# A hashed attention with a max-of-three feed-forward: new costs in the build-time planner, and weights sent on other queues

## The chip, the core and the metric

The kernel runs on one core of a Trainium2 chip. The core has a matrix engine (TensorE, PE in the profile, with its weight loads as PEld), a vector engine (VectorE, DVE), an activation engine (ScalarE, ACT), GpSimd (POOL) and SyncE (SP), which here only issues DMA transfers. Each engine runs its own instructions strictly in the order in which the program holds them, and waits for the others by semaphores. An instruction that waits therefore holds up everything behind it on its engine. DMA transfers are issued from the queue of SyncE, ACT or POOL. The metric is the time of one execution in microseconds (us), as the median of several runs.

## The reference

Two computations follow each other. The first is attention with a hashed mask: a key counts for a query only if six sign bits agree.

```python
q_bits = (np.einsum('bhsd,dk->bhsk', q, proj) > 0)      # q, k, v: 4 x 8 x 768 x 64
k_bits = (np.einsum('bhsd,dk->bhsk', k, proj) > 0)      # proj: 64 x 6
q_bucket, k_bucket = sum(q_bits * powers), sum(k_bits * powers)
mask = q_bucket[:, :, :, None] == k_bucket[:, :, None, :]
scores = np.where(mask, q @ k.T / 8, -1e9)
attn = softmax(scores)
x = (attn @ v)        # heads side by side: 3072 tokens x 512
h = np.maximum(np.maximum(x @ w1, x @ w2), x @ w3)      # w1, w2, w3: 512 x 768
out = h @ w_out                                          # w_out: 768 x 512
```

All inputs and the output are float32. Where no key shares a query's bucket, the softmax is over equal values, so that the mean of v is what is left; the kernel adds a tiny share of that mean everywhere.

## The kernel before

**Tiles and stages.** A batch b has eight heads, handled in four pairs. A pair is written (b, pr) here, so (1,3) is the fourth pair of the second batch. For each pair the kernel loads q, k and v (`load`, 384 KB each), splits q and k into a half-precision part and its remainder (`split_h`, `split_r`), and brings both into the layout that scores need, the tile T. Batch 0 and the first two pairs of batch 1 do this with TensorE (`pe_T`, `evac_T`), all others with one transposing DMA from SyncE (`xbar`, L271). From T come the sign bits: small matmuls with the projection (`hash_mm`, L298 or L300), a comparison (`hash_bits`), a transpose of the bits (`bit_T`, `bit_evac`), and a round trip through DRAM (`bit_out` L337, `bit_in` L340) that writes the bits as extra rows into T. These rows, scaled by a large number, act as the mask inside the score matmul itself. A pair's scores can thus start only after its `bit_in` has landed.

The attention of one head and half a sequence takes three units, each of two score matmuls (`score`, L383), one exponential on ACT (`expo`, L389) and six matmuls with v (`attend`, L401). Division and placement are DVE's (`norm_t` L418, `norm_x` L437). `mean_mm` (L361, L364) makes the mean of v. For b = 0 it sums the half-precision v; for later batches POOL sums v first (`vsum`, L351 to L354). `vcast` makes v half-precision, for batch 0 on POOL (L193), later on ACT (L191).

The feed-forward works on half a batch, (b, hf). The half's x is transposed (by TensorE for the first half, else by one transposing DMA, `x_bar`, L445). Then come 18 groups of four matmuls (`l1`, L466), whose results ACT and DVE take from PSUM (`l1_evac`, L191, L193, L475), and three chunks of six matmuls with w_out (`l2`, L480), each copied (`l2_evac`) and stored (`store`, L489). This work fills TensorE while ACT works on the exponentials of the following batches, and what is left runs on its own at the end.

**Weights.** w1, w2, w3 are loaded by casting DMAs from POOL's queue, half by half (`load_w`, L523), w_out by one such DMA (L638). `weights` gives their places: the first halves early, the second half of w1 after pair (0,3), of w2 and w3 after pair (1,0), w_out after pair (1,1). A `hold` instruction on POOL makes them wait until that pair's bit rows have landed.

**The order of the work.** It is not written by hand. `Plan.run` simulates the engines while the program is built: every step has engines with costs, a priority (mostly the number of the unit that needs it), dependencies and the buffers that it takes and gives back. At each moment a free engine takes the ready step with the lowest priority number, and the step's instructions are emitted in that order. DMA transfers stand in one queue: a transfer occupies it for `xfer` us, after the issuing engine's cost and a lead time, and counts as landed 1.2 us after that. A transposing DMA costs SyncE 2.0 us (`xbar`) or 1.4 us (`x_bar`), with 4.3 or 2.1 us of queue. Where the planner is wrong, the order stays as it was built, and the engines wait.

**Gates and buffers.** The loads of later pairs are also gated: they are planned after the `bit_in` of a given earlier pair (`g` in `prep`). The pools that matter are T (8 buffers, pool `opnd`), the output tiles (3, `osb`), the exponentials (5, `at`) and three PSUM banks (`mm`) that nearly all other matmuls share.

Of the kernel before, what the change touches and what calls it, by code (L numbers as in the profile page):

```python
# [18 lines left out]
class Task:  # L19
    def __init__(self, kinds, prio, deps, emit, take=(), give=(), after=(), lat=0.0, xfer=0.0):  # L20
        self.kinds, self.prio, self.emit = kinds, prio, emit
        self.deps = [d for d in deps if d is not None]
        self.take, self.give, self.lat, self.xfer = take, give, lat, xfer
        self.after = [t for t in after if t is not None]
        self.start = None


class Plan:
# [17 lines left out]
    def run(self):  # L46
# [11 lines left out]
        while n < len(self.tasks):  # L58
            moved = True
            while moved:  # L60
                moved = False
                for e in engines:
# [22 lines left out]
                    events.append((busy[e], -1, None))  # L85
                    if t.xfer:
# [16 lines left out]
            while queue and queue[0][0] < 1e-6:  # L103
                t = queue.pop(0)[1]
                events.append((now + POST, t.n, t))
            events.sort(key=lambda x: x[:2])
            while events and events[0][0] <= now:
                at, kind, t = events.pop(0)
                if kind == -2:
                    queue.append([t.xfer, t])  # L110
                    continue
# [12 lines left out]
def kernel(  # L124
# [39 lines left out]
    OSB = 3  # L164
# [4 lines left out]
    opnd = ctx.enter_context(tc.tile_pool(name="opnd", bufs=8))  # L169
# [5 lines left out]
    hp = ctx.enter_context(tc.tile_pool(name="hp", bufs=HT))  # L175
    op = ctx.enter_context(tc.tile_pool(name="op", bufs=OSB))
# [7 lines left out]
    plan = Plan({"sc": 2, "av": 1, "mm": 3, "at": 5, "q": 4, "k": 4, "v": 4, "s": 4, "T": 8,  # L184
                 "xn": XN, "xT": XT, "ht": HT, "osb": OSB, "bit": 2, "bt": 2, "dr": 4, "t": 2})
# [102 lines left out]
    def hash_mm(b, pr, heads, e):  # L288
        hps = bank(("h", b, pr), "hps")
        K = NBITS if b == 0 else 2 * NBITS  # L290
        for n in range(2):
            for hh in range(*heads):
                for c in range(NCH):
                    a = n * NA2 + hh * NCH + c
                    o = hps[:, a * K : (a + 1) * K]
                    if b == 0:
# [179 lines left out]

    def l2(b, hf, c, e):
        ps = bank(("o", b, hf, c), "po")
        for fb in range(NF):
            nc.tensor.matmul(ps[:], hts[b, hf, fb][:, c * P : (c + 1) * P], wout_sb[:, fb, :],  # L480
                             start=fb == 0, stop=fb == NF - 1)

    def l2_evac(b, hf, c, e):
        osbs[b, hf, c] = op.tile([P, DM], FP32, tag="osb", name="osb")
        copy(e, osbs[b, hf, c][:], pss.pop(("o", b, hf, c))[:])

    def store(b, hf, c, e):
        rows = out[b * S : (b + 1) * S, :].rearrange("(p c) m -> p c m", c=NCH)
        nc.sync.dma_start(rows[:, hf * CH + c, :], osbs.pop((b, hf, c))[:])  # L489
# [36 lines left out]
    last_load, last_copy = [None], [None]  # L526
    bounced = {}

    def value(b, pr, dep):
# [5 lines left out]
        else:  # L535
            ready_v[b, pr] = add(("ACT", 0.72), U - 6, [dep, prev], lambda e: vcast(b, pr, e))
# [5 lines left out]
    def prep(b, pr):  # L542
# [3 lines left out]
        if b > 0:  # L546
            for n in "qkv":
                g = divmod(4 * b + pr - GATE, 4)
                if b == 1:
                    g = {("q", 0): (0, 2), ("k", 0): (0, 2), ("q", 2): (1, 0), ("k", 2): (1, 0), ("v", 2): (1, 0)}.get(  # L550
                        (n, pr), (0, 3) if pr < 2 else (1, 1))
                loads[n, b, pr, (0, 2)] = add(("SP", 0.5), U - 44 + 0.1 * "qkv".index(n), [],
                                              lambda e, n=n: load(n, b, pr, (0, 2), e), take=(n,), xfer=1.1,
                                              after=[last_load[0], bounced[g]])
# [46 lines left out]
        if not by_pe:  # L601
            ev = [add(("SP", 2.0), p0 + 2, both_rs, lambda e: xbar(b, pr, e), xfer=4.3, take=("T",))]
        plan.join(ev, ("s",))
        hm = add(("PE", 1.3 if b == 0 else 0.67), p0 + 4, ev + [mp], lambda e: hash_mm(b, pr, (0, 2), e), take=("mm",))
        hb = add(("DVE", 0.3 if b == 0 else 0.62), p0 + 5, [hm],
                 (lambda e: hash_bits(b, pr, e)) if b else (lambda e: hash_bits0(pr, (0, 2), e)), take=("bit",), give=("mm",))
# [22 lines left out]

    def weights(b, pr, parts):  # L630
        if pr or b:
            prev = add(("POOL", 0.1), -150, [bounced[b, pr]], lambda e: hold(b, pr, e), after=[wprev[0]])
        else:
            prev = ready_v[0, 1]
        for w in parts:
            if w == "o":
                prev = add(("POOL", 0.8), -90, [],
                           lambda e: nc.gpsimd.dma_start(wout_sb[:], moe_w_out.rearrange("(c p) m -> p c m", p=P)),  # L638
                           xfer=4.6, after=[prev])
# [6 lines left out]
    stage = {(0, 3): [(1, 0)], (1, 0): [(1, 1), (1, 2)], (1, 1): ["o"]}  # L646

    def ffn(b, hf, deps):
# [16 lines left out]
        for c in range(CH):  # L665
# [94 lines left out]
```

The softmax here doesn't subtract the row's maximum and nothing guards it: scores larger than these inputs give would overflow.

## Time and profile before

| | |
|---|---|
| median of 6 runs | 275.71 us (274.5 to 277.77) |
| the profiled execution | 274.5 us |
| its span, first to last instruction | 272.7 us |
| TensorE busy | 259.9 us, 95% |
| ACT busy | 195.9 us, 72% |
| DVE busy | 175.0 us, 64% |
| POOL busy | 38.6 us, 14% |
| mean granted TensorE clock | 0.990 |
| moved by DMA | 40.51 MB, in 67,216 packets |

The profile is of one execution. Busy time of TensorE is not time at its peak, since matmuls overlap: the start of one 384-column matmul to the next is 162 ns in dense stretches, while a group's mean length is given as 327. A DMA share can exceed 1 in the table of stretches; read it as a queue that is never empty. SyncE has no busy time of its own: its timeline shows how long each issue held it. Of the words in a wait, the right side is what came last. The granted clock is the share of the full TensorE clock that the chip allows.

### The profile page before, as it was taken

What the parts mean: (1) busy time and instruction counts of PE and PEld (TensorE: products, weight loads), DVE (VectorE), ACT (ScalarE), POOL (GpSimd) and SP (SyncE); (2) the same over time, 40 slices, a digit from 0 to 9 for tenths busy, and PEclk for the clock granted to TensorE, in tenths of its full rate; (3) what the DMA queues carried; (4) which work ended last, traced back from release to release, by engine and by line L of the source; (5) the groups of instructions that cost most, each with busy time, mean ns of one, the idle gap of its engine ahead of it and who ended that gap; (6) DMA issues with size and microseconds to landing.
All of it is one profiled execution on the core that took longest, in us unless ns stands there. A gap on an engine that the chain in (4) does not pass through costs nothing.

```text
span 272.7 us, 7413 instructions
## 1 busy us (share of the span) xinstructions
PE 259.9 (95%) x3034; PEld 174.9 (64%) x3034; DVE 175.0 (64%) x392; ACT 195.9 (72%) x282; POOL 38.6 (14%) x56
## 2 busy tenths in 40 slices
PE   7899989999999699899999999999999999999993
PEld 7778767667656365567666676666666656565551
DVE  4898588959958578667999466464356715354350
ACT  5788899989856178899999889998889432322322
POOL 1170043604303033030333000000000000000000
PEclk9999999999999979999999999999999999999998
DMA  6995496799999979998899950211250060120303
GB/s 199 370 232 90 142 277 192 122 155 335 190 299 226 164 233 225 265 236 238 198 208 218 239 116 8 30 30 41 77 60 4 0 168 8 40 79 0 115 0 117
DMA packets 67216, 40.51 MB, mean 149 GB/s; under 512 B 47982, under 2 KB 64110, under 8 KB 67182
## 3 DMA queue, kind: packets, MB, share of 16 engines
q1 hardware_dynamic: 63150, 36.90, 55.3%
q0 software_dynamic: 3952, 3.15, 7.8%
q8 instruction: 23, 0.38, 0.6%
q14 instruction: 11, 0.09, 0.1%
q10 hardware_dynamic: 80, 0.00, 0.0%
HBM read 25.72 MB, written 6.84 MB: 119 GB/s over the span
## 4 chain that ended last, share of the span: by engine, by line
PE 75%; DMA 9%; DVE 7%; ACT 4%; issue 2%; SPq 1%; ACTq 0%
PE ps L466 32%; PE sc L383 19%; PE av L401 10%; PE po L480 10%; ACT AT L389 3%; DMA q<-in_q_dram 3%; DMA T<-s 3%; DVE s L262 3%; DMA T<-dr 3%; PE hps L300 2%; DVE s L257 2%; PE tps L281 1%; PE hps L298 1%; DVE T L193 1%; ACT s L255 1%
## 5 line engine op out<-in xcount | busy, mean ns | idle before, releaser
L389 ACT ACTIVATE AT<-sc 128x768 f16<-128x768 f32 x192 | 146.0, 812 | 16.0 <-PE sc L383 15.1
L466 PE MATMUL ps<-xT,w_sb 128*128 128x384 f16 x576 | 107.1, 327 | 0.7 <-ACT ht L191 0.6
L383 PE MATMUL sc<-T 128*128 128x384 f16 x384 | 93.8, 328 | 3.2 <-DMA T<-dr 1.9
L475 DVE TENSOR_TENSOR ht<-ht,ps 128x384 f16<-128x384 f16 x96 | 53.0, 552 | 47.0 <-PE ps L466 43.5
L401 PEld LDWEIGHTS <-AT 128*128 128x128 f16 x1152 | 60.1, 98 | 24.2 <-issue 1.1
L466 PEld LDWEIGHTS <-w_sb 128*128 128x128 f16 x576 | 52.4, 98 | 31.0 <-issue 1.5
L401 PE MATMUL av<-vone,AT 128*128 128x65 f16 x1152 | 66.3, 194 | 0.2 <-DVE t L418 0.2
L383 PEld LDWEIGHTS <-T 128*128 128x128 f16 x384 | 30.1, 97 | 14.2 <-DMA T<-dr 2.5
L191 ACT CAST ht<-ps 128x384 f16<-128x384 f32 x30 | 14.4, 478 | 32.8 <-DVE ht L475 20.6
L480 PE MATMUL po<-wout_sb,ht 128*128 128x512 f16 x144 | 33.4, 379 | 0.1
L191 ACT COPY osb<-po 128x512 f32<-128x512 f32 x23 | 13.5, 585 | 18.6 <-PE po L480 18.5
L480 PEld LDWEIGHTS <-ht 128*128 128x128 f16 x144 | 13.6, 98 | 14.7 <-issue 0.2
L351 POOL TENSOR_TENSOR vt<-v 128x384 f32<-128x384 f32 x12 | 13.4, 1117 | 63.5 <-DMA v<-in_v_dram 63.4
L418 DVE TENSOR_TENSOR t<-av,mv 128x390 f32<-128x390 f32 x32 | 17.9, 560 | 6.7 <-PE av L401 6.7
L262 DVE SCALAR_TENSOR_TENSOR s<-k,s 128x384 f16<-128x384 f32 x32 | 20.5, 653 | 0.7 <-ACT s L255 0.5
L262 DVE SCALAR_TENSOR_TENSOR s<-q,s 128x384 f16<-128x384 f32 x32 | 18.2, 582 | 3.3 <-ACT s L255 3.1
L193 DVE CAST ht<-ps 128x384 f16<-128x384 f32 x18 | 10.0, 555 | 15.1 <-PE ps L466 15.0
L437 DVE TENSOR_TENSOR xn<-t,rr 128x384 f16<-128x384 f32 x32 | 18.9, 591 | 1.1
L281 PE MATMUL tps<-iden,s 128*128 128x128 f16 x168 | 13.4, 219 | 1.6 <-DVE s L262 0.8
L281 PEld LDWEIGHTS <-s 128*128 128x128 f16 x168 | 10.4, 97 | 3.1 <-DVE s L262 2.2
L191 ACT CAST vone<-v 128x768 f16<-128x768 f32 x12 | 10.0, 837 | 0.3 <-DMA v<-in_v_dram 0.3
L300 PEld LDWEIGHTS <-T 128*128 128x128 f16 x288 | 8.7, 96 | 1.7 <-DMA T<-s 0.8
(53 smaller groups left out, 141.3 us busy)
## 6 DMA issues: line engine op xcount, KB each, us to landing
v<-in_v_dram SPq DMA_DIRECT2D x16, 384.0 KB
out_dram<-osb SPq DMA_DIRECT2D x24, 256.0 KB
q<-in_q_dram SPq DMA_DIRECT2D x15, 384.0 KB
k<-in_k_dram SPq DMA_DIRECT2D x15, 384.0 KB
w_sb<-in_moe_w_dram POOLq DMA_DIRECT2D x6, 384.0 KB, 6.8
wout_sb<-in_moe_w_out_dram POOLq DMA_DIRECT2D x1, 768.0 KB, 11.0
dr<-bt SPq DMA_DIRECT2D x15, 36.0 KB
T<-dr SPq DMA_DIRECT2D x15, 36.0 KB
```

The source lines that it names most:

```text
L191: nc.scalar.copy(o, i)
L262: nc.vector.scalar_tensor_tensor(out=s[:, a0:a1, D : 2 * D], in0=raw_view(n, b, pr, heads), scalar=QS, in1=s[:, a0:a1, 0:D], op0=AluOp.mul ...
L281: nc.tensor.transpose(p16[:, c * P : (c + 1) * P], S16[b, pr][:, a0 + c, :], iden[:])
L300: nc.tensor.matmul(o, T[b, pr][:, a, :], PAB[:], start=True, stop=True)
L383: nc.tensor.matmul(sc[:, i, 0:HQ], t[:, NA2 + hh * NCH + 2 * j + i, :], t[:, hh * NCH + hf * CH : hh * NCH + (hf + 1) * CH, :], start=True ...
L389: nc.scalar.activation(AT[:], scs.pop(u)[:, :, 0:HQ], ActFn.Exp, bias=EXP_BIAS, scale=EXP_SCALE)
L401: nc.tensor.matmul(av[:, o : o + D + 1], AT[:, i, c * P : (c + 1) * P], vones[b % 2][:, 2 * pr + hh, 2 * j + i, 0 : D + 1], start=slot == ...
L418: nc.vector.tensor_tensor(out=t[:, :, :, 0 : D + 1], in0=av[:, :, :, 0 : D + 1], in1=mv, op=AluOp.add)
L437: nc.vector.tensor_tensor(out=xv, in0=t[:, :, :, 0:D], in1=rr[:].to_broadcast([P, 2, CH, D]), op=AluOp.mult)
L466: nc.tensor.matmul(ps[:, 0:HQ], w_sb[i][:, jc, fb * P : (fb + 1) * P], xTs[b, hf][:, jc, :], start=jc == 0, stop=jc == NJ - 1)
L475: nc.vector.tensor_tensor(out=ht[:], in0=ht[:], in1=ps[:, 0:HQ], op=AluOp.max)
L480: nc.tensor.matmul(ps[:], hts[b, hf, fb][:, c * P : (c + 1) * P], wout_sb[:, fb, :], start=fb == 0, stop=fb == NF - 1)
```

## The change

The diff has six parts.

1. The planner knows a `hold`: a step with it keeps its engine (SyncE) until the transfer has reached the head of the queue and run for `hold` us. Transposes of T are now 0.6 us of issue, 3.4 of hold and 4.6 of queue, those of x 0.6, 1.0 and 2.3. Loads of a pair are planned only after the transpose of the pair two before it.
2. The gates of batch 1's loads move: those of pair (1,2) are now planned right behind those of (1,1). The second halves of w1 and w2 follow pair (0,3), that of w3 pair (1,0).
3. w_out is no longer cast by a DMA. SyncE loads it in three pieces of 512 KB in float32 into two new buffers (`wst`), and POOL casts them.
4. `vcast` of batch 1 is done by POOL instead of ACT.
5. The hash of pair (0,3) uses the form that batches 1 to 3 have: one matmul with both parts of the projection and a comparison of two columns, instead of two accumulating matmuls.
6. The last chunk of w_out is computed, copied and stored in two halves of 256 columns. T has 6 buffers instead of 8, and the output has 4 instead of 3.

```diff
@@ Plan.run
-                    events.append((busy[e], -1, None))
-                    if t.xfer:
+                    if t.hold:
+                        busy[e] = 1e9
+                        events.append((now + dur, -2, t))
+                    else:
+                        events.append((busy[e], -1, None))
+                    if t.hold:
+                        pass
+                    elif t.xfer:
...
-                t = queue.pop(0)[1]
+                t, hold = queue.pop(0)[1:]
+                if hold:
+                    busy[t.engine] = now
+                    queue.insert(0, [t.xfer - t.hold, t, 0.0])
+                    continue
...
-    OSB = 3
+    OSB = 4
-    opnd = ctx.enter_context(tc.tile_pool(name="opnd", bufs=8))
+    opnd = ctx.enter_context(tc.tile_pool(name="opnd", bufs=6))
+    wst = ctx.enter_context(tc.tile_pool(name="wst", bufs=2))
@@ hash_mm
-        K = NBITS if b == 0 else 2 * NBITS
+        summed = 4 * b + pr < 3
+        K = NBITS if summed else 2 * NBITS
@@ value
-            ready_v[b, pr] = add(("ACT", 0.72), U - 6, [dep, prev], lambda e: vcast(b, pr, e))
+            ready_v[b, pr] = add(("POOL", 0.9) if b == 1 else ("ACT", 0.72), U - 6, [dep, prev], lambda e: vcast(b, pr, e))
@@ prep
-                    g = {("q", 0): (0, 2), ("k", 0): (0, 2), ("q", 2): (1, 0), ("k", 2): (1, 0), ("v", 2): (1, 0)}.get(
-                        (n, pr), (0, 3) if pr < 2 else (1, 1))
+                    g = {("q", 0): (0, 2), ("k", 0): (0, 2)}.get((n, pr), (0, 3) if pr < 3 else (1, 0))
...
-                                              after=[last_load[0], bounced[g]])
+                                              after=[last_load[0], bounced[g], xbars.get(4 * b + pr - 2)])
...
-            ev = [add(("SP", 2.0), p0 + 2, both_rs, lambda e: xbar(b, pr, e), xfer=4.3, take=("T",))]
+            ev = [add(("SP", 0.6), p0 + 2, both_rs, lambda e: xbar(b, pr, e), xfer=4.6, hold=3.4, take=("T",))]
+            xbars[4 * b + pr] = ev[0]
@@ weights
+    def stage_w(w, i, e):
+        from_dram = w_view(w, i)[0]
+        t = wst.tile([P, 2 * DM], FP32, tag="ws", name="ws")
+        wst_tiles[w, i] = t[:, 0 : 2 * from_dram.shape[2]].rearrange("p (c f) -> p c f", c=2)
+        nc.sync.dma_start(wst_tiles[w, i], from_dram)
+
+    def cast_w(w, i, e):
+        copy(e, w_view(w, i)[1], wst_tiles.pop((w, i)))
...
-                prev = add(("POOL", 0.8), -90, [],
-                           lambda e: nc.gpsimd.dma_start(wout_sb[:], moe_w_out.rearrange("(c p) m -> p c m", p=P)),
-                           xfer=4.6, after=[prev])
+                for i in range(NF // 2) if w == "o" else range(NJ // 2):
+                    ld = add(("SP", 0.5), -60 if w == "o" else -70, [], lambda e, w=w, i=i: stage_w(w, i, e), take=("ws",),
+                             xfer=1.4 if w == "o" else 1.1, after=[prev])
+                    prev = ld
+                    parts.append(add(("POOL", 1.5 if w == "o" else 1.1), -60, [ld], lambda e, w=w, i=i: cast_w(w, i, e),
+                                     give=("ws",)))
...
-    stage = {(0, 3): [(1, 0)], (1, 0): [(1, 1), (1, 2)], (1, 1): ["o"]}
+    stage = {(0, 3): [(1, 0), (1, 1)], (1, 0): [(1, 2)], (1, 1): ["o"]}
@@ ffn
-        for c in range(CH):
+        for c in range(CH) if (b, hf) != (B - 1, 1) else (0, 1, 2.1, 2.6):
@@ main loop
-                    lst = [add(("SP", 1.4), u, lst, lambda e, b=b, hf=hf: x_bar(b, hf, e), xfer=2.1, take=("xT",),
+                    lst = [add(("SP", 0.6), u, lst, lambda e, b=b, hf=hf: x_bar(b, hf, e), xfer=2.3, hold=1.0, take=("xT",),
```

## The prediction

> **What bounds the kernel now.** I read four views in this order: busy time by engine, busy time by stretch, the SyncE timeline, the chain.
>
> ```profile
> PE 259.9 (95%) x3034; PEld 174.9 (64%) x3034; DVE 175.0 (64%) x392; ACT 195.9 (72%) x282; POOL 38.6 (14%) x56
> ```
>
> TensorE is the bound: 95% busy, and what it still lacks is the prize. Nothing after 120 us leaves it idle (below), so an idle microsecond removed before that is a microsecond off the end. The stretches (start:end, then busy us of PE, weight loads, DVE, ACT, POOL; granted clock; DMA share; GB/s) say where it idles:
>
> ```profile
> 24.00:60.00 36.00, 34.44 (x522) 25.43 (x519) 27.87 (x66) 33.80 (x48) 10.15 (x14) 1.00 0.71 162
> 60.00:88.00 28.00, 28.00 (x324) 18.39 (x323) 21.92 (x49) 21.94 (x32) 8.02 (x11) 1.00 1.13 262
> 88.00:96.00 8.00, 5.41 (x48) 3.07 (x46) 4.30 (x12) 0.96 (x2) 0.00 (x0) 1.00 1.08 182
> 96.00:100.00 4.00, 4.00 (x47) 2.52 (x45) 3.40 (x6) 2.81 (x5) 1.54 (x2) 0.58 0.52 161
> 100.00:116.00 16.00, 14.88 (x183) 9.51 (x181) 11.95 (x28) 13.92 (x20) 2.92 (x5) 1.00 1.08 257
> 116.00:160.00 44.00, 43.88 (x594) 30.51 (x593) 34.24 (x78) 39.86 (x57) 9.12 (x12) 1.00 1.04 222
> ```
>
> Between 88 and 96 PE lacks 2.6 us and ACT stands nearly still (0.96 of 8 busy); then the granted clock is 0.58 for 4 us, another 4.00 x 0.42 = 1.7 us. From 100 to 116 it lacks 1.1 us, from 24 to 60 1.6 us beside an almost full ACT. DMA is saturated from 60 to 160 (shares over 1) and slack before (0.71). Why 88 to 96 stalls stands in the SyncE timeline (start, length):
>
> ```profile
> 68.74 6.91 SPq L271 DMA_TRANSPOSE T<-s  x1
> 75.75 0.42 SPq L340 DMA_DIRECT2D T<-dr  x1
> ...
> 78.27 6.16 SPq L271 DMA_TRANSPOSE T<-s  x1
> ...
> 86.69 3.74 SPq L271 DMA_TRANSPOSE T<-s  x1
> 90.54 0.41 SPq L340 DMA_DIRECT2D T<-dr  x1
> ```
>
> and in the chain (start, length):
>
> ```profile
> 90.54 4.98 DMA T<-dr
> 95.56 0.82 PE sc L383 x4
> ...
> 102.58 8.24 DMA T<-s
> 110.86 0.76 PE hps L300 x24
> ```
>
> A transpose holds SyncE for 3.7 to 6.9 us where the planner books 2.0. The bit rows of pair (1,3), which the next scores need, were issued behind transpose (2,1): SyncE was free at 90.5, and the rows landed behind the transpose's packets at 95.5.
>
> **The change part by part.** Sums are against the profiled execution: 272.7 us of span, 274.5 us in all.
>
> *New order on SyncE.* The planner now books 0.6 + 3.4 us of hold behind whatever is queued, and 4.6 us of queue. In the built order the rows of (1,3) go out ahead of transpose (2,1), behind stores only: the 2.6 + 1.7 us of that stall can go, 4.3. The wait at 110 (hash of (2,2) behind its transpose) goes too, since that transpose now has nothing but the transpose of x (1,0) and three loads close ahead of it: 1.1 of 100 to 116. The order pays earlier: in front of the rows of (1,2) now stand transposes (1,3), x (0,1) and (2,0), where (2,0) used to follow. What makes that fit is that the loads of (1,2) and (1,3) move up into the slack at 33 to 56, so transpose (1,3) is asked for some 9 us of the queue earlier. Late next are, in TensorE's order, x (0,1) before the first product of the second half, the rows of (1,2), then of (1,3): each just in time. I book 0.5 for them, bounds 0 (all arrive) and 4 (a copy of today's stall).
>
> *Six T buffers instead of eight.* Transpose (2,2) now waits for the last scores of (1,0), (2,3) for those of (1,1). Behind them in SyncE's queue stand the rows of (2,1), the loads of (3,0) and the stores of half (0,1). The rows are wanted some 15 us later and a fourth output buffer takes the stores: nothing, unless TensorE itself is late, and then its delay is already counted. Up to 1 us otherwise.
>
> *Hash of pair (0,3) in one pass.* 48 small matmuls become 24: the chain has "PE hps L298 x48" at 1.18 us and L300 x24 at 0.58, so 0.6 us less PE. DVE does L318 + L320 (0.30 + 0.31) instead of L308 (0.30), 0.3 more, under that stretch's other waits.
>
> *Casts of v of batch 1 from ACT to POOL.* ACT loses 4 x 0.84 = 3.3 us in a stretch where it has 33.8 of 36; of the 1.6 us PE idles there I give back 0.5 (0 to 1.6). POOL takes 4 x 0.97 us (L193, same tile), and its sums of v (1.12 + 0.62 + 0.58 with gaps, 2.5 us) queue behind: 3.5 us a pair after v lands, and TensorE has the means of (1,1) and (1,2) in its in-order queue with scores, transposes and products behind them.
>
> When does v land? The planner lets transfers land in order of arrival, with the two weight halves behind all three loads of (1,2). The Trainium skill, "DMA: Bandwidth & Descriptors", Queues, rings and completion order, says otherwise: each DMA engine takes turns between the queues that have work, packet by packet. The trace sides with it: with one weight transfer in flight k of (1,1) landed 2.79 us after q, 39.88 against 37.09, where undisturbed loads land 1.05 apart. Now two are in flight together. By the planner's rule v (1,2) is there before its mean is due: no loss. By turns, v (1,1) lands at about 41.5 and v (1,2) at about 47: from 39.9, four loads x 1.05 and some 3 left of two weights x 2.2 (the spacing of the first three, alone). The means follow 3.5 us later, at 45 and 50.5. In the built order they stand behind the 31st and the 36th score, which today run at about 43 and 48; the first wait of 2 shifts the second, so 2 to 2.7 us in all. Part replaces idle that is there now; I book 1.8, bounds 0 and 3.
>
> *DVE beside a busier POOL.* Added POOL work: 4 x 0.97 plus three casts of w_out, 1024 columns each, estimated 0.97 x 1024/768 = 1.29: 7.8 us. Sorting DVE's instructions by overlap with POOL arithmetic: L262 of k takes 901 ns beside POOL and 548 alone, L437 796 and 558, while L475, which reads PSUM, takes 545 and 553. The Trainium skill, "SBUF — State Buffer", Who interferes with whom, calls it an exclusive lock: a DVE instruction with two SBUF inputs blocks until the POOL one ends. By the lock at its worst each of seven casts costs DVE its length, 7.8 us; by the rows some 6 exposed instructions lose 0.35 each, 2.1 us. I take the rows. DVE has 27.9 of 36 in that stretch and its late steps are waited for together with the means: 0.5 on the path, 0 to 2.
>
> *w_out plain.* Today one casting DMA from POOL, 62.95 to 73.95, with its first use at 74.4. Now three SyncE loads (0.45 us of issue each; 512 KB at 1.05 per 384 KB, 1.4 us of queue) and the casts. Two loads stand before the loads of (2,0), which move back by 2.8 us and are not wanted before transpose (2,0); the third waits behind transpose (1,3), a buffer to be cast and POOL's sum of (2,0). It lands about 73 to 74, is cast by 76, and the first w_out product comes after 76: nothing, or a first-use wait of 1 inside the 0 to 4 above.
>
> *Last chunk in halves.* ACT's last copy (0.58) becomes a half: 585 ns at 512 columns and 478 at 384 make 107 per 128, so 0.37: 0.2 less. Twelve weight loads of 98 ns stay just under matmuls of 108.
>
> Sum: gains 4.3 + 1.1 + 0.6 + 0.5 + 0.2 = 6.7; losses 0.5 + 1.8 + 0.5 = 2.8; net 3.9. The profiled run would take 270.6. It was the fastest of the six; on the median, 275.7, that is 271.8.
>
> **The rivals.** *All goes in* (chance 0.2): the waits for the means fall into idle time that exists anyway, the new order arrives everywhere: 275.7 - 6.3 = 269.4. For it: 1.6 us of idle at 24 to 60. Against: DVE and ACT are full there. *The stall only moves* (0.17): the queue is saturated from 60 on, and one more transpose stands before the rows of (1,2), so at 73 to 88 TensorE waits 3 us of the 4.3 saved: 275.7 - 1 = 274.7. It is also what is seen if the new costs reorder without removing a wait. *Slower* (0.15): the transposes (1,3), x (0,1), (2,0) run back to back, each booked 4.6 or 2.3 us, while today's held SyncE 6.9 and 6.2; if the rows behind them arrive 6 us late at 73 to 82, the idle costs 6 plus 1.7 of clock, and with 1.8 + 0.5 from before it 10.0 against gains of 6.7: 275.7 + 3.3 = 279.0. With the clock lost it breaks even at a wait of 2.7 us and passes 1% at 5.5.
>
> **How the numbers follow.** The likeliest case (0.48) has 270 to 273.5 as its own range. Within 1% of 275.7, about what a measurement can tell, is 272.9 to 278.5. Faster by more: 0.41 of the likeliest case and 0.19 of the first rival, 0.60. Slower by more: 0.12 of the last rival's 0.15. The rest, 0.28, is the same. The range 268.8 to 276.5 leaves out half the first rival's better end and most of the last.
>
> **What would show it.** Right: the chain has no T<-dr of 5 us near 90, granted clock 1.00 between 88 and 104, no wait of hps for T<-s near 110; instead PE waits of 1 to 2 us at svp near 43 to 51, ps after xT near 75, sc near 80. L262 means go up. ACT's vone casts fall from 12 to 8. Wrong: idle PE of more than 4 us between 70 and 90, a clock below 1.00 there, or a first w_out product waiting for its cast.

## The result, and the profile after

| | before | after |
|---|---|---|
| median | 275.84 us (73 runs) | 273.89 us (36 runs, 271.62 to 278.09) |
| ratio, with its 95% interval | 1 | 0.9915 [0.9895, 0.9936] |
| profiled execution | 274.5 us | 273.85 us |
| its span | 272.7 us | 272.0 us |
| mean granted TensorE clock | 0.990 | 0.998 |

The change makes the kernel 0.85% faster, 2.3 us of 275.84, where the forecast was 3.9 us. The sign was right and the time lies inside the range, but by the bound of 1% this counts as "within 1%", which had been given only 0.28. The ratios, here and below, use only executions within 1.5% of a kernel's fastest, which leaves out 13 of 37 of after and 4 of the 48 of before that ran beside the kernels below, so a ratio can differ a little from the quotient of two medians.

The busy times of after:

```profile
PE 257.4 (95%) x3016; PEld 174.8 (64%) x3016; DVE 175.0 (64%) x389; ACT 195.6 (72%) x283; POOL 46.3 (17%) x61
```

POOL has gained 7.7 us. The seven casts were booked at 7.8 and take 6.9 (3.8 for v, 3.1 for w_out); most of the rest is that its sums of v take 1.4 us longer in all. TensorE has lost 2.5 us of busy time; a part of that is the slow clock that is gone, since a matmul at 0.58 of the clock counts as busy for longer. The stretches of after, with the columns as before:

```profile
24.00:60.00 36.00, 31.62 (x478) 23.68 (x477) 30.08 (x68) 31.24 (x44) 16.80 (x21) 1.00 0.80 184
60.00:88.00 28.00, 25.97 (x311) 17.18 (x308) 19.04 (x42) 18.74 (x29) 7.76 (x9) 1.00 1.01 252
88.00:96.00 8.00, 7.17 (x80) 4.78 (x79) 6.09 (x15) 6.13 (x9) 0.66 (x1) 1.00 0.93 238
96.00:100.00 4.00, 3.84 (x39) 2.49 (x38) 4.00 (x9) 3.84 (x6) 1.67 (x3) 1.00 1.02 254
100.00:116.00 16.00, 15.98 (x223) 11.15 (x221) 10.76 (x28) 14.74 (x21) 2.33 (x3) 1.00 0.92 195
116.00:160.00 44.00, 42.58 (x541) 28.76 (x539) 33.13 (x72) 38.85 (x57) 9.94 (x12) 1.00 0.88 208
```

The hole at 88 to 96 is nearly closed (7.17 of 8 instead of 5.41), the clock behind it is 1.00 instead of 0.58, and 100 to 116 is full. But three stretches have new or larger holes: 24 to 60 (34.44 before), 60 to 88 (28.00 before) and 116 to 160 (43.88 before). The waits of TensorE between 36 and 160 us name them (waiting instruction, what came last, us in total, times, longest):

```profile
PE hps L312 <- DMA T<-s: 2.0, 1, 2.0
PE sc L395 <- ACT AT L401: 1.6, 2, 1.4
PE tps L292 <- DVE s L273: 1.1, 2, 0.8
PE svp L376 <- POOL vsum L366: 1.0, 1, 1.0
PE sc L395 <- DMA T<-dr: 0.8, 1, 0.8
```

Before, the first line of that list was the score's wait for its rows, 1.9 us.

For a balance of the whole I took, from the trace, the time from the start of each matmul to the start of the next, less what that kind takes in dense stretches (163 ns for 384 columns, 31 for an `av`, 27 for an `hps`, and so on). What is left is time that TensorE lacked, slow clock included, in us:

| stretch | before | after | difference |
|---|---|---|---|
| 0 to 40 | 7.06 | 8.09 | +1.0 |
| 40 to 60 | 2.20 | 3.71 | +1.5 |
| 60 to 88 | 0.31 | 2.44 | +2.1 |
| 88 to 100 | 4.75 | 1.46 | -3.3 |
| 100 to 116 | 2.16 | 0.34 | -1.8 |
| 116 to 160 | 0.78 | 2.17 | +1.4 |
| 160 to the end | 0.61 | 0.63 | 0.0 |

To this come 0.65 us less work of the hash, and 1.07 us less between TensorE's last matmul and the end of the span: -0.75 in all, beside -0.68 for the two spans. The rows from 40 to 160 us sum to -0.1: what the new order saved, 5.1 us, came back elsewhere as 5.0. What is left of the gain in this pair is the shorter hash and the shorter end, 1.7 us, two edits that had been booked at 0.8. One pair can't settle these shares for the medians, since executions of one kernel differ by more than that.

The first row is mostly no effect of the change. Up to the hash of (0,3), near 29 us, TensorE's order is the same, and before 30 us this execution of before lacked 5.1 us, that of after 6.3; in ten of the twelve kernels below it was 5.9 to 6.4 as well (5.0 and 5.6 in two). So the one profiled execution of before was ahead by about 1.1 us, which the pair shows as less gain than the medians.

**The stall that went.** SyncE of after (start, length), around the rows of pair (1,3):

```profile
83.96 0.32 SPq L349 DMA_DIRECT2D dr<-bt  x1
84.39 4.09 SPq L507 DMA_DIRECT2D out_dram<-osb  x2
88.58 0.32 SPq L352 DMA_DIRECT2D T<-dr  x1
...
90.96 5.18 SPq L282 DMA_TRANSPOSE T<-s  x1
```

The rows (L352) go out ahead of the transpose, as the prediction read it from the built order. They stand behind two stores instead, and the second one waits for its tile. The chain (start, length):

```profile
87.30 0.13 PE bps L339 x2
87.43 0.68 DVE osb L204
88.11 0.02 issue
88.13 0.34 SPq L507
...
88.58 2.77 DMA T<-dr
91.36 0.05 issue
91.40 0.50 PE sc L395 x2
```

The bits had been in DRAM since 87.25; a copy of 0.68 us and a store stood before `bit_in`, and TensorE waited 0.8 us. This is one of the three just-in-time arrivals that had 0.5 booked together.

**The wait in the hash.** The chain between 40 and 66 us:

```profile
34.97 6.52 DMA v<-in_v_dram
41.49 0.05 issue
41.55 0.82 POOL vone L204
42.37 1.30 POOL vt L363
...
43.74 0.66 POOL vt L365
...
44.47 0.87 POOL vsum L366
45.34 0.04 issue
45.38 0.22 PE svp L376
...
52.41 11.39 DMA T<-s
63.81 0.05 issue
63.85 0.76 PE hps L312 x24
```

The upper part is as predicted: v of (1,1) landed at 41.49 (predicted 41.5), its mean followed at 45.38 (45), v of (1,2) landed at 46.86 (47). The lower part was not predicted at all: the transpose of (1,2) took 11.39 us from issue to landing, and the hash of that pair waited 2.0 us for it. At 52.34, just before the issue, POOL had sent the second half of w3, which landed at 59.71.

**The wait behind a cast.** ACT between 117 and 125 us (start, length; the idle time before it in brackets):

```profile
117.56 1.49 ACT L401 ACTIVATE AT<-sc 128x768 f16<-128x768 f32 x2
120.69 0.83 ACT L202 CAST vone<-v 128x768 f16<-128x768 f32 x1 [1.64 <-DMA v<-in_v_dram]
121.43 0.58 ACT L202 COPY osb<-po 128x512 f32<-128x512 f32 x1
121.91 2.96 ACT L401 ACTIVATE AT<-sc 128x768 f16<-128x768 f32 x4
```

ACT stood 1.64 us before the cast of v of (3,0), whose load was issued at 114.25 and landed at 120.61. The exponentials behind it came late, and the next score waited 1.4 us for ACT. That load was late in part because SyncE, from 107.36 to 108.97, waited for scores to free a T buffer for the transpose ahead of it:

```profile
109.01 3.66 SPq L282 DMA_TRANSPOSE T<-s  x1
...
114.25 0.41 SPq L250 DMA_DIRECT2D v<-in_v_dram  x1
```

**The end.** The chain of before ends so, and that of after below it:

```profile
264.51 3.90 PE po L480 x18
...
268.47 0.58 ACT osb L191
```

```profile
264.88 3.91 PE po L496 x24
...
268.86 0.37 ACT osb L202
```

The copy is 0.21 us shorter, as booked. But from its end to the end of the span it is 2.82 us instead of 3.68 (272.05 less 269.23; 272.73 less 269.05): the store of half the bytes is over 0.86 us sooner, which the prediction left out.

### The profile page after: what moved, and what is told of

Its sections match the earlier page's. It is cut to its first block, busy times and chain, and to the rows that moved or that the text cites. A ratio compares the mean times of both kernels' runs of the same rounds, so it can differ in the third digit from the quotient of the medians.

```text
span 272.0 us, 7378 instructions
## 1 busy us (share of the span) xinstructions
PE 257.4 (95%) x3016; PEld 174.8 (64%) x3016; DVE 175.0 (64%) x389; ACT 195.6 (72%) x283; POOL 46.3 (17%) x61
## 4 chain that ended last, share of the span: by engine, by line
PE 71%; DMA 15%; DVE 5%; ACT 2%; SPq 2%; issue 1%; POOL 1%; ACTq 0%
PE ps L478 32%; PE sc L395 17%; PE po L496 10%; PE av L413 9%; DMA v<-in_v_dram 5%; DMA T<-s 4%; DMA dr<-bt 2%; DVE s L273 2%; PE hps L312 2%; DMA T<-dr 2%; DMA q<-in_q_dram 2%; ACT AT L401 2%; SPq L250 1%; DVE T L204 1%; DVE s L268 1%
## 5 line engine op out<-in xcount | busy, mean ns | idle before, releaser
L487 DVE TENSOR_TENSOR ht<-ht,ps 128x384 f16<-128x384 f16 x96 | 52.9, 551 | 44.6 <-PE ps L478 41.5
L413 PE MATMUL av<-vone,AT 128*128 128x65 f16 x1152 | 65.5, 193 | 0.0
L395 PEld LDWEIGHTS <-T 128*128 128x128 f16 x384 | 30.4, 97 | 15.5 <-DMA T<-dr 2.4
L202 ACT CAST ht<-ps 128x384 f16<-128x384 f32 x32 | 15.3, 479 | 30.0 <-DVE ht L487 19.1
L496 PE MATMUL po<-wout_sb,ht 128*128 128x512 f16 (+1 forms) x150 | 33.5, 371 | 0.0
L202 ACT COPY osb<-po 128x512 f32<-128x512 f32 (+1 forms) x22 | 12.4, 566 | 17.1 <-PE po L496 17.0
L273 DVE SCALAR_TENSOR_TENSOR s<-q,s 128x384 f16<-128x384 f32 x32 | 21.7, 687 | 3.4 <-ACT s L266 3.1
L273 DVE SCALAR_TENSOR_TENSOR s<-k,s 128x384 f16<-128x384 f32 x32 | 19.3, 618 | 0.6 <-ACT s L266 0.4
L204 DVE CAST ht<-ps 128x384 f16<-128x384 f32 x16 | 8.9, 553 | 5.6 <-PE ps L478 5.1
L312 PE MATMUL hps<-PAB,T 128*128 128x12 f16 x312 | 9.7, 168 | 2.0 <-DMA T<-s 2.0
L312 PEld LDWEIGHTS <-T 128*128 128x128 f16 x312 | 9.2, 96 | 3.0 <-DMA T<-s 2.1
```

The lines of the kernel that those rows point to most:

```text
L202: nc.scalar.copy(o, i)
L273: nc.vector.scalar_tensor_tensor(out=s[:, a0:a1, D : 2 * D], in0=raw_view(n, b, pr, heads), scalar=QS, in1=s[:, a0:a1, 0:D], op0=AluOp.mul ...
L312: nc.tensor.matmul(o, T[b, pr][:, a, :], PAB[:], start=True, stop=True)
L395: nc.tensor.matmul(sc[:, i, 0:HQ], t[:, NA2 + hh * NCH + 2 * j + i, :], t[:, hh * NCH + hf * CH : hh * NCH + (hf + 1) * CH, :], start=True ...
L413: nc.tensor.matmul(av[:, o : o + D + 1], AT[:, i, c * P : (c + 1) * P], vones[b % 2][:, 2 * pr + hh, 2 * j + i, 0 : D + 1], start=slot == ...
L487: nc.vector.tensor_tensor(out=ht[:], in0=ht[:], in1=ps[:, 0:HQ], op=AluOp.max)
```

## The experiments

The theory after the result: the gain comes from the order on SyncE, and what is missing of it went into two new waits, for the transpose of (1,2) beside the weight half, and for POOL's sums of v behind its casts. The rivals: the new costs alone do it; the new gates or weight places do; the casts do more harm than the waits show; plain w_out counts. Two rivals were not tested by a kernel of their own: that the shorter hash and the halved last chunk alone make most of the gain, as the balance says, and that eight T buffers would do better than six. Each kernel is compared with before, run beside it on the same chip. Intervals are some 0.6% to either side, so two kernels must lie 1% apart to be told apart.

**e1_costs_only.** The kernel before with only the planner's new costs and its `hold`.

```diff
-            ev = [add(("SP", 2.0), p0 + 2, both_rs, lambda e: xbar(b, pr, e), xfer=4.3, take=("T",))]
+            ev = [add(("SP", 0.6), p0 + 2, both_rs, lambda e: xbar(b, pr, e), xfer=4.6, hold=3.4, take=("T",))]
...
-                    lst = [add(("SP", 1.4), u, lst, lambda e, b=b, hf=hf: x_bar(b, hf, e), xfer=2.1, take=("xT",),
+                    lst = [add(("SP", 0.6), u, lst, lambda e, b=b, hf=hf: x_bar(b, hf, e), xfer=2.3, hold=1.0, take=("xT",),
```

> The kernel before with the new costs of transposes alone (hold of SyncE, queue time); gates, weights, w_out, casts and buffers as before. Theory A, the new costs are what removed the stall at 88 to 96: the time falls by most of the 4.3 us that stall cost, to a ratio of 0.985 to 0.99 of the kernel before. Theory B, the gain came from the earlier loads, which bring transpose (1,3) and then the rows of (1,3) forward, and the costs alone only reorder: in the built order the rows of (1,3) still stand behind transpose (2,1), so a wait for rows of 3 us or more stays between 85 and 97 and the ratio is 0.995 to 1.005.

Measured: 274.85 us, 0.9953 [0.9912, 0.9994]. The stretch 88 to 100 lacks 0.78 us instead of 4.75, so the costs do take the stall away; but 60 to 88 lacks 1.79 instead of 0.31, 116 to 160 2.16 instead of 0.78, and the early stretches more as well. The costs alone move the stall and keep little: the time is that of theory B, the trace that of A. In all, this trace lacks as much TensorE time as that of after; the 1.8 us between the two spans (273.8 and 272.0) are the hash and the end, which e1 doesn't have.

**e2_cut_weights.** The order of after; of the second halves of w1, w2 and w3 only a quarter is loaded, the rest is set to zero.

```diff
-        nc.gpsimd.dma_start(w_sb[i][:, :, f], w_ap[:, :, f])
+        n = 1 if half else NJ
+        nc.gpsimd.dma_start(w_sb[i][:, 0:n, f], w_ap[:, 0:n, f])
```

> The changed kernel in the same order, but the second halves of w1, w2 and w3 are loaded only to a quarter (one of four row blocks; the other blocks are set to zero on POOL at the start). What it leaves out is DMA traffic between 36 and 60 us, no instruction of any engine after the start. Theory A, the weight transfers take turns with the loads of v and q and with transpose (1,2), and so make the waits for the means at 44 and for the transpose at 62: v of (1,2) lands 3 to 4 us earlier, both waits shrink to under 0.5 us each, and the time falls by 2 to 3 us against the changed kernel, to a ratio of 0.981 to 0.985 of the kernel before. Theory B, the waits come from POOL and DVE being slower than planned there: the time falls by under 1 us (0.988 to 0.992).

Measured: 272.06 us, 0.9897 [0.9838, 0.9955]. TensorE's waits between 40 and 72 us have no line of the hash any more, and none of `svp`:

```profile
PE tps L294 <- DVE s L275: 1.2, 2, 0.9
PE bps L341 <- DVE bit L334: 0.5, 1, 0.5
PE ps L480 <- DVE bt L346: 0.3, 1, 0.3
```

The transpose of (1,2), issued at 51.81, held SyncE for 4.32 us instead of 7.79 and landed at 57.93 instead of 63.81. The three loads ahead of the transpose landed 2.5 us earlier too, so not all of the 5.9 us is the weight half's doing (e8 says more). The scores' wait for the rows of (1,3) near 88 is 1.1 us instead of 0.8. The ratio fell in the range of theory B and can't be told from that of after.

One part of theory A failed: v of (1,2) landed at 46.31 instead of 46.86, not 3 to 4 us earlier, and v of (1,1) at 40.68 instead of 41.49, with three quarters of both weight transfers gone. The `svp` wait needed only these 0.8 us and somewhat shorter sums to go.

**e3_cut_casts.** The order of after; POOL casts only a sixth of v in batch 1 (so v of batch 1 is left out for the most part; other batches are not touched).

```diff
-        copy(e, vones[b % 2][:, 2 * pr : 2 * pr + 2, :, 0:D],
+        n = 1 if b == 1 else NCH
+        copy(e, vones[b % 2][:, 2 * pr : 2 * pr + 2, 0:n, 0:D],
```

> The changed kernel in the same order, but POOL's four casts of v of batch 1 write only one of six column blocks (the rest of that tile is set to 1 on POOL at the start, so attention of batch 1 and 3 uses wrong values). What it leaves out is some 3.5 us of POOL time between 37 and 58 us. Theory A (DMA turns): the wait for the means falls by about 0.8 us a pair at the most, transpose (1,2) still lands at about 63, and the time falls by under 1 us (0.988 to 0.992). Theory B (POOL's casts and the DVE instructions that they slow): the waits at 42 to 51 go, L273 of q falls from 687 ns towards 582, the transpose is asked for and lands 2 us earlier, and the time falls by 2 us or more (0.982 to 0.985).

Measured: 274.75 us, 0.9882 [0.9791, 0.9973]: on the time, nothing settled. The transpose landed at 61.03, but was also issued 2 us earlier and took 10.66 us. In the trace the two lines that count stay:

```profile
PE hps L315 <- DMA T<-s: 1.3, 1, 1.3
PE svp L380 <- POOL vsum L370: 1.0, 1, 1.0
```

The cast is down to 0.29 us, and from v's landing to the end of its sum it takes 3.31 us (39.98 to 43.29) instead of 3.85 (41.49 to 45.34). The cast is 0.5 us of that path, and the three sums are nearly all the rest. TensorE was also 2 us earlier there, so the wait is as long as in after.

**e4_act_casts.** After, with the casts of batch 1 on ACT again, planned anew.

```diff
-            ready_v[b, pr] = add(("POOL", 0.9) if b == 1 else ("ACT", 0.72), U - 6, [dep, prev], lambda e: vcast(b, pr, e))
+            ready_v[b, pr] = add(("ACT", 0.72), U - 6, [dep, prev], lambda e: vcast(b, pr, e))
```

> The changed kernel with the casts of v of batch 1 on ACT as before, the order planned anew. If POOL's casts cost more than they free on ACT, it is faster than the changed kernel by 0.5 to 2 us (0.984 to 0.99 of the kernel before); if ACT's 3.3 us matter, it is slower by 1 us or more (0.995 or above). DVE's mean for L273 of q is back to 580 to 620 ns in either case.

Measured: 271.55 us, 0.9810 [0.9735, 0.9885]. No wait for POOL's sums is left between 36 and 72 us. ACT is full again from 24 to 60, and TensorE does more there, not less:

```profile
24.00:60.00 36.00, 33.88 (x513) 25.25 (x511) 31.05 (x72) 33.96 (x49) 11.97 (x17) 1.00 0.83 195
```

The time is below both expected ranges. So in this plan the relief of ACT was worth nothing: with ACT at 33.96 of 36, TensorE's waits for it between 36 and 72 us are 0.3 us. Whether the casts on POOL cost time in the end is taken up with e12.

**e5_old_stage.** After, with the second halves of w2 and w3 behind pair (1,0) again.

```diff
-    stage = {(0, 3): [(1, 0), (1, 1)], (1, 0): [(1, 2)], (1, 1): ["o"]}
+    stage = {(0, 3): [(1, 0)], (1, 0): [(1, 1), (1, 2)], (1, 1): ["o"]}
```

> The changed kernel with the weights in their old places: one second half after pair (0,3), two after pair (1,0); order planned anew. If transfers on two queues take turns, the waits move with the weights: v of (1,1) lands about 1 us earlier and TensorE no longer waits for the mean at 44, but two halves instead of one now run beside transpose (1,2), which is asked for at about 52 and lands at 65 or later instead of 63.8, with a wait of 3 us or more in its hash. Sum: 0 to 2 us slower than the changed kernel, 0.991 to 0.998 of the kernel before. If weights and loads don't disturb each other, nothing changes by more than 0.5 us (0.989 to 0.994) and the transpose lands at 63 to 64.

Measured: 278.62 us, 1.0112 [1.0048, 1.0176], slower than before. Both halves were sent at 50.42 and 51.21, ahead of the transpose at 52.10, which landed at 63.27. TensorE waited 2.82 us for it, and the clock behind that wait is low:

```profile
58.00:62.00 4.00, 2.50 (x31) 1.67 (x28) 2.55 (x7) 2.84 (x4) 0.00 (x0) 1.00 1.15 209
62.00:66.00 4.00, 2.68 (x42) 2.01 (x43) 0.61 (x2) 0.96 (x2) 1.15 (x2) 0.60 1.06 349
66.00:70.00 4.00, 4.00 (x24) 2.18 (x23) 2.18 (x5) 2.18 (x3) 1.86 (x2) 0.55 1.14 311
```

The stretch 60 to 88 lacks 6.08 us. At 137 ACT stood 3.07 us before a cast of a late v, and TensorE 2.4 us behind it. The time missed both expected ranges, and two details of turn-taking failed: with one half fewer beside its load, v of (1,1) landed only 0.55 us earlier (40.94) and TensorE still waited 1.0 us for its mean; with one more beside it, the transpose landed no later than in after.

**e6_wout_pool.** After, with w_out loaded by the one casting DMA of before.

```diff
+            if w == "o":
+                prev = add(("POOL", 0.8), -90, [],
+                           lambda e: nc.gpsimd.dma_start(wout_sb[:], moe_w_out.rearrange("(c p) m -> p c m", p=P)),
+                           xfer=4.6, after=[prev])
```

> The changed kernel with w_out loaded by one casting DMA from POOL as before (no staging tiles, no casts on POOL), order planned anew. The prediction gave the staged w_out no price: within 0.5 us of the changed kernel (0.989 to 0.994). If the casting DMA is the costlier one, by its turns with transpose (1,3) and x (0,1), it is slower by 1 to 2 us with a wait in l1 or l2 at 74 to 80 (0.995 to 1.0). If SyncE's three loads or POOL's casts cost, it is faster by 1 us or more (below 0.988).

Measured: 273.07 us, 0.9900 [0.9822, 0.9977], not to be told from after: no price of plain w_out shows, and one above some 0.8% is excluded. (In after its last cast ended at 77.1 and the first product with w_out came at 81.0.)

**e7_old_gates.** After, with the loads of batch 1 gated as before.

```diff
-                    g = {("q", 0): (0, 2), ("k", 0): (0, 2)}.get((n, pr), (0, 3) if pr < 3 else (1, 0))
+                    g = {("q", 0): (0, 2), ("k", 0): (0, 2), ("q", 2): (1, 0), ("k", 2): (1, 0), ("v", 2): (1, 0)}.get(
+                        (n, pr), (0, 3) if pr < 2 else (1, 1))
```

> The changed kernel with the old gates of batch 1's loads (those of (1,2) after pair (1,0), those of (1,3) after (1,1)); order planned anew. Theory: the earlier loads are what let the rows of (1,3) go out before transpose (2,1). In the built order they do still go out after one transpose more than in the changed kernel, so the stall at 85 to 97 comes back in part (2 us or more of idle TensorE there) while the waits for the means at 44 are gone: 0.993 to 1.0 of the kernel before. If the gates don't matter it stays at 0.989 to 0.994.

Measured: 278.91 us, 1.0127 [1.0062, 1.0191], slower than before. The transpose of (1,2) is issued at 59.86 instead of 52.41 and lands at 70.44. From 36 to 72 us the means wait for POOL three times:

```profile
PE svp L376 <- POOL vsum L366: 3.2, 3, 1.9
PE tps L292 <- DVE s L273: 1.1, 3, 0.7
```

and 100 to 116 lacks 3.25 us, 116 to 160 4.07. Both parts of the expectation were missed: the waits for the means grew instead of going, and 88 to 100 lacks 1.8 us. The transpose took 10.6 us with no weight half beside it, but two pieces of w_out and three loads had been sent from SyncE in the 2.5 us before it.

**e8_act_early.** The casts on ACT as in e4, and all three second halves sent behind pair (0,3).

```diff
-    stage = {(0, 3): [(1, 0), (1, 1)], (1, 0): [(1, 2)], (1, 1): ["o"]}
+    stage = {(0, 3): [(1, 0), (1, 1), (1, 2)], (1, 1): ["o"]}
```

> The changed kernel with the casts of v of batch 1 on ACT and all three second halves sent after pair (0,3), so that no weight transfer is left beside transpose (1,2); order planned anew. With turn-taking as the cause of the late transpose it lands by 60, no wait in its hash, but the loads of (1,2) and (1,3) land later. I expect 0 to 1 us faster than with the casts on ACT alone: 0.977 to 0.982 of the kernel before. If the transpose is late for another reason, it is the same or slower, 0.981 to 0.988.

Measured: 270.76 us, 0.9835 [0.9776, 0.9893], the lowest median of all. The last half landed at 51.28, the transpose was issued at 54.17 and landed at 59.74, 5.57 us later, and no hash waits. The last of the three loads ahead of it landed as late as in after (56.32 and 56.05), so this shows more cleanly than e2, and without work left out, that the weight half made the transpose late: without it, it landed 4.1 us sooner. The time is no better than that of e4, where 0 to 1 us had been expected. 116 to 160 still lacks 3.1 us.

**e9_no_costs.** After, with the planner's old costs of transposes and no `hold`: e1's diff turned round.

> The changed kernel with the old costs of transposes (2.0 and 1.4 us of SyncE, 4.3 and 2.1 us of queue, no hold), everything else as changed; order planned anew. In the built order the rows of (1,3) still go out ahead of transpose (2,1). Theory, after the two earlier runs: gates and weights remove the stall at 88 to 96, the costs add little. Then it is within 1 us of the changed kernel (0.988 to 0.995 of the kernel before), with under 2 us of idle TensorE between 88 and 100. If the costs are needed beside the gates, a wait for rows or for a transpose of 3 us or more stands between 70 and 125, and the ratio is 0.998 or above.

Measured: 271.24 us, 0.9834 [0.9763, 0.9905]. Without the new costs the changed kernel is no slower. Its trace, of its longest execution (274.79 us), has no wait for the rows of (1,3), but lacks 2.5 us between 88 and 100, where under 2 were expected.

**e10_swap.** The casts of batch 1 on ACT, those of batches 2 and 3 on POOL, so that ACT stands behind no late v.

```diff
-            ready_v[b, pr] = add(("POOL", 0.9) if b == 1 else ("ACT", 0.72), U - 6, [dep, prev], lambda e: vcast(b, pr, e))
+            ready_v[b, pr] = add(("ACT", 0.72) if b == 1 else ("POOL", 0.9), U - 6, [dep, prev], lambda e: vcast(b, pr, e))
```

> The changed kernel with the casts of v the other way round: batch 1 on ACT, batches 2 and 3 on POOL; order planned anew. If ACT, standing in order behind a cast whose v has not landed, is what makes TensorE wait 1.6 us near 121, that wait goes and the two waits for v at 42 to 51 go too: 0.975 to 0.981 of the kernel before. If the wait only goes over to another step, it equals the run with all casts on ACT, 0.981 to 0.986.

Measured: 274.24 us, 0.9941 [0.9893, 0.9990]. TensorE's wait for ACT is down to 0.3 us between 36 and 160, but another has come:

```profile
PE svp L376 <- POOL vsum L366: 3.5, 6, 1.2
PE av L413 <- DVE t L430: 1.4, 3, 0.8
```

The time is worse than both expectations. The cast stands before the sums on POOL; the wait went over from the exponentials to the means.

**e11_swap_early.** e10 with e8's weight places.

> The same casts (batch 1 on ACT, later ones on POOL) and all three second halves sent after pair (0,3). It should join the two gains: no wait for transpose (1,2) near 62 and none for ACT's cast near 121 to 129, TensorE's idle time after 52 us under 5 us. 0.974 to 0.981 of the kernel before; if the order planned anew makes new waits of 1 to 2 us instead, 0.981 to 0.986.

Measured: 271.13 us, 0.9845 [0.9784, 0.9906]. Its waits for POOL's sums are 0.9 us instead of 3.5, its trace lacks 15.3 us in all (after 18.8), and its profiled span is 268.5 us. In the time it can't be told from e8.

**e12_act_no_costs.** e4 with the planner's old costs.

> The changed kernel with both parts taken back that have shown no gain by themselves: the casts of v of batch 1 on ACT again, and the planner's old costs of transposes (2.0 and 1.4 us of SyncE, 4.3 and 2.1 of queue, no hold). What stays of the change is the earlier loads, the earlier weight halves, the plain w_out and the small edits. Theory (earlier loads and weights make the gain, casts on POOL cost some 1%, new costs are worth nothing): the ratio is that of the kernel with the casts on ACT or below, 0.975 to 0.985, some 269 to 271.5 us; TensorE does not wait for POOL's sum of v, and the rows of pair (1,3) are there within 1.5 us of being wanted. Rival (the casts on ACT need the new costs, since ACT is later and the planner must know how long SyncE is held): the old stall near 88 comes back, 3 us or more of idle at 88 to 100, and the ratio is 0.99 or above.

Measured: 272.67 us, 0.9893 [0.9833, 0.9953], between the two expectations. The rival's stall did not come back (88 to 100 lacks 1.15 us), and the ratio is not the one that the theory gave. With after, e4 and e9 it makes a square:

| | casts of batch 1 on POOL | on ACT |
|---|---|---|
| new costs | 0.9915 (after) | 0.9810 (e4) |
| old costs | 0.9834 (e9) | 0.9893 (e12) |

On the mean of its two kernels each side stands at 0.9863 (new costs) against 0.9864 (old), and at 0.9875 (POOL) against 0.9852 (ACT). Each edit makes the planner build another order, and neither edit has an effect of its own that can be seen; with intervals of 0.6 to 0.75% for three of the four, part of the differences is chance. That the casts on POOL cost 1%, which e4 alone seemed to say, is not shown.

What all these kernels agree in: with the new gates and the second halves of w1 and w2 sent early, whatever else, the ratio is 0.98 to 0.994; with one of the two taken back it is above 1.01. Each of the latter is one plan, so this shows that neither can be taken back alone, and not that the two together make the gain: e1, with both old, stands at 0.9953. Two versions beat before and after by intervals that don't touch: e4, and e8 (270.76 us), which also has no wait for the transpose. As two of twelve, and e8 by a hair, they should be measured again. Of the two, e8 is the one whose trace says why, as far as that wait goes.

## Why the prediction was right or wrong

The sign, the stall that would go and the order on SyncE were right. Of 3.9 us 2.3 came, and that this is so near is in part luck: in the profiled pair the new waits ate what the new order saved, and the gain stands on the hash and the end; and of what the order saved there, 1.7 us are a fall of the clock that most executions of before don't have (last section). In that, the rival "the stall only moves" came nearer. Step by step, from the profiled pair:

- **New order on SyncE.** Booked 4.3 and 1.1, measured 3.3 (88 to 100, with the rows of (1,3) 0.8 us late in it) and 1.8 (100 to 116): 5.1 of 5.4. The prediction took the new costs and the earlier loads together for its cause. Either takes most of the stall away without the other: 88 to 100 lacks 0.8 us in e1, with the costs alone, and 1.15 in e12, without them. Two things were read too simply. Of the 2.6 us of idle time only 1.9 were a wait for the rows; 0.6 were a wait of `ps` for ACT at 89.4. And the 1.7 us of slow clock were taken from the one profiled execution, while only 11 of 48 of before show such a fall.
- **Late next.** Booked 0.5 for three arrivals. One of them, the rows of (1,3), was late, by 0.8, and not behind a transpose but behind a store that waited for a copy.
- **Transpose of (1,2).** This is the step that failed. The prediction looked for what is late behind the transposes at 73 to 82, and let the weight halves delay only the loads of v; it applied the turns of the queues to v and not to the transpose 10 us later, which shares them with the half of w3. It cost 2.1 us (60 to 88), with no price in the sum. e2, e8 and e11 take the weight out of its way, and the wait is gone in all three. The Trainium skill, "DMA: Bandwidth & Descriptors", Queues, rings and completion order, which the prediction used, covers this case too: each DMA engine takes turns between the queues that have work. In after, in the two stretches of 2 us from 54 to 58, the packets of POOL's queue took 59% and 94% of the 16 DMA engines' time, and those of SyncE's, with the transpose among them, 46% and 51%.
- **Means behind late v.** Booked 1.8, with 0.5 for DVE and 0.5 back from ACT: 1.8. Measured 1.5 from 40 to 60: 1.0 for `svp`, 0.8 for a late part of a split (`tps`), the rest in small waits. The arrivals were right within 0.4 us, but not shown to be so for the stated reason: e2 cut the two weight transfers to a quarter and v landed only 0.8 and 0.55 us earlier. The second mean had no wait.
- **DVE beside POOL.** Part of the same 1.5. Split instructions (L273) that lie mostly beside POOL's arithmetic take 964 (q, ten of them) and 729 ns (k, eleven) against 551 and 547 alone. Over the lone times all of L273 together lost 6.6 us, where before had lost 4.4 (L262): 2.2 us more of DVE work against the 2.1 booked, part of it off the path. A full block behind each of the seven casts would have been 7.8.
- **Relief of ACT.** Booked a gain of 0.5; e4 shows none, in its own plan.
- **ACT behind a late v.** Not booked: 1.4 us at 121. The prediction looked at six T buffers and found only rows and stores behind the waiting transpose; the loads of (3,0) stood there too, it said so, and then followed only the rows. SyncE waited until 109.0 for a T buffer and issued v at 114.25, and ACT, in order, had the cast of that v in front of exponentials. That the buffers are the cause is argued from the trace (SyncE's 1.6 us for the buffer, ACT's 1.64 for v) and not tested: before and e1, with eight buffers, have no such wait over 0.3 us, while after and its variants have one of 0.6 to 2.4 us behind 100, unless POOL does the later casts (e10, e11).
- **Hash, w_out, end.** 0.6 booked and 0.65 measured; 0 and 0 (e6); 0.2 booked and 1.07 measured, since the last store is shorter as well.

The sum: from the booked -3.9, two waits without a price (+2.1 and +1.4), 0.9 more at the end and some 0.5 better in the other rows lead to -1.8, where the medians have -1.95 and the ratio -2.3. The profiled pair, with -0.65, shows less, about by the 1.1 us by which that execution of before was ahead in the first 30 us. (The first rival's 6.3 does not come out of its terms: 6.7 less 0.5 for DVE is 6.2. Nothing hangs on it.)

## What to carry to other kernels

When a transfer is moved earlier, list everything that will be in flight beside it, transposes first, and give each a price, not only the transfer that the engine waits for today. Where an order comes from a planner, two edits that are each harmless can build a good order together and a bad one singly, so judge them in pairs and by more than one plan. Sum up what the waits gained and lost before crediting a gain to the order; in the profiled pair two small edits stood behind it. Before booking a stretch of slow clock as a gain, see in how many executions it occurs. An engine that works in order should get no step that waits for a transfer ahead of steps that others need: moving the cast from one engine to another only chose who stands behind it.

## What the runs showed of the hardware

The transpose of pair (1,2), from issue to landing by the trace's semaphores. A weight half is a casting load of 384 KB from POOL's queue; "behind v" is the part after the last of the q, k and v loads ahead of it had landed:

| in flight beside it | runs | issue to landing, us | behind v, us |
|---|---|---|---|
| a half issued 0.1 to 1.1 us before it (e5: two) | after, e3, e5, e6, e9 | 11.4, 10.7, 11.2, 11.5, 9.1 | 7.8, 6.6, 9.7, 8.6, 5.8 |
| a half issued 3.1 us before it | e4, e10, e12 | 7.5, 7.4, 5.6 | 6.9, 5.6, 5.4 |
| none (e8, e11), or a quarter of one (e2) | e8, e11, e2 | 5.6, 6.0, 6.1 | 3.4, 4.7, 4.4 |
| none, but two pieces of w_out and three loads sent 0.5 to 2.5 us before it | e7 | 10.6 | 2.7 |
| no loads ahead (e1: the tail of a half) | before, e1 | 6.8, 6.7 | |

A load that takes some 2 us of the queue when alone thus went with a transpose that was some 4 to 5 us later if both started together, and SyncE was held for 6.7 to 7.8 us instead of 3.8 to 4.3. The weight is not the only thing that does this: in e7 SyncE's own queue held five transfers, and SyncE was held for 8.5 us.

The granted clock did not follow the length of a stall. It fell after single stalls of TensorE of 1.9 us (before, at 95.6), 2.0 us (e6, at 63.9) and 2.8 us (e5, at 63.3), and stayed at 1.00 after 2.0 us (after, at 63.9), 1.9 us (e7, at 46.8) and twice 2.4 us (e9, at 45.9; e5, at 138.6). The stalls of after and of e6 are the same wait in the same place, and only behind that of e6 the clock is low:

```profile
64.00:68.00 4.00, 4.00 (x48) 2.55 (x49) 1.38 (x4) 1.88 (x3) 1.71 (x3) 0.58 1.21 260
```

A fall cost 4.00 x 0.42 = 1.7 us in before and in e6, and 4.00 x (0.40 + 0.45) = 3.4 us in e5.

So a fall belongs to an execution. One lowers the mean clock by 1.7/272.7 = 0.006. Of the 48 executions of before that ran beside the kernels above, 37 have a mean of 0.996 or more, with no room for a fall other than the one behind the last matmuls, and took 275.1 us on the average; 11 have 0.994 or less, and took 277.2. Of 37 of after it is 20, with 273.0 us, and 17, with 275.8. The profiled pair has it the other way round: there before has the fall and after has none.
